# The last two pairs of heads of a stage share a matrix product, and the first pair of the next stage moves three products ahead

## The chip, the core and the metric

The kernel runs on one core of a Trainium2 chip. The metric is the device time of one execution in microseconds (us); lower is better. The core has a matrix engine (TensorE, PE in the profile; its weight loads are shown apart as PEld), a vector engine (VectorE, DVE), a scalar engine (ScalarE, ACT), GpSimd (POOL, idle here) and SyncE (SP), whose queue issues all DMA transfers. The engines run side by side and wait for each other through semaphores; within one engine the instructions run in the order in which the program lists them.

## What is computed

```python
# attention: q, k, v of shape (8, 12, 448, 64); sigmoid in place of softmax
scores = scale * q @ k.T - log(S)
attn_out = sigmoid(scores) @ v
x = attn_out, heads joined: (8 * 448, 768)
# feed-forward (FFN)
h = x @ w_in                     # 768 -> 2048
g = maximum(0.01 * h, h)
out = g @ w_out                  # 2048 -> 768
```

The weights arrive as 64-bit numbers and are turned to 32-bit ones on the chip.

## The kernel before

**Attention.** The 12 heads of 8 batches are handled as 48 pairs of heads, 12 pairs (two batches) to a stage; a pair's two heads sit on partitions 0 to 63 and 64 to 127. `Pair.scores(h)` (L336) makes two of four chunks of the transposed scores, in three matmuls for each head, since every operand of a product is split into a high and a low part; ScalarE applies the sigmoid to each chunk. `Pair.attn_v(h)` (L359) multiplies two chunks by v into one bank of the accumulator memory (PSUM), and `keep` (L379) copies the result into `xs`, where the 12 pairs of a stage fill four quarters `x(0)` to `x(3)` of three pairs each.

**Alone or joint.** `part(i)` (L40) says how the 448 keys of a pair are cut. Part 0, alone: four chunks of 112 rows, so v takes 8 matrix products. Parts 1 and 2 are two neighbouring pairs taken jointly: three chunks of 128 rows each, and the last 64 rows of both pairs sit in one tile, the first pair's on the lower and the second's on the upper partitions. The second pair's `attn_v(1)` (L369) makes the four small products of the shared tile for both pairs, and both pairs' `keep` come after it. In each of the stages 1 to 3 the pairs 0 to 9 of the stage are joint and the pairs 10 and 11 alone (`JOINT`, L36). In a trace each of these products stands as two matmuls.

**FFN, first half.** `First(p)` (L472) multiplies the result of attention stage p by `w_in`. Rows and columns are halved, and seven products (n = 0, 1, 4, 5, 3, 6, 2) of sums and differences of the halves take the place of eight; for eight column groups u that makes 56 products p0 to p55, of nine matmuls each. While stage q of the attention runs (q = 1 to 3), these are the products of stage q - 1; those of the last stage follow alone. Product n of group u accumulates in one of two PSUM banks, `px` and `pz`; `First.after` and `Quad.done` (L191) empty the bank by a copy on ScalarE (n = 0, 4, 5, 2) or an addition on VectorE (n = 1, 3, 6), and the product after next needs that bank. In the group u = 7 the sums of n = 3 and 2 are in `pz` and that of n = 6 is in `px`; n = 0 of the next group begins in `px`.

**Operands.** `Operands` (L385) makes the seven left operands from `x(0)` to `x(3)`: `s` entries are sums or differences on VectorE, `h` entries casts on ScalarE, `l` entries the differences that leave the low part, on VectorE. `PLAN` (L433) says ahead of which slot each comes: "h422" is the cast for product 4, pairs 2 to 2 of the quarter; "np2" is product 2 of the next stage. The weights of a product are cast by ScalarE three products ahead and get their low part from VectorE two products ahead (`advance`, L453).

**Slots.** `slot` (L112) first issues the chores that are due, those marked `first` ahead, and then the slot's matrix work; `later(n, ...)` puts a chore n slots on. `go` (L552) adds the entries of the plans, and, unless `busy` is set, `prepare` lets the conversion of the weights on VectorE (`prep`, L246) go one or two instructions on. With a pair come the casts of q and k of the pair after next, the load of v of the next pair, and a load of q and k for the pair four on (`next_parts`, L545).

**Order in a stage.** Ahead of each pair's slot run e{j}.0 (half its scores), e{j}.1 and e{j}.2 (v of the pair before it), e{j}.3 (the other half), and then 5, 5 or 4 products:

```python
            go(q, f"e{j}.0", (lambda: pairs[i].scores(0)) if q < NQ else None, busy)
            for h in range(2):
                go(q, f"e{j}.{1 + h}", lambda: pairs[i - 1].attn_v(h), busy)
            go(q, f"e{j}.3", (lambda: pairs[i].scores(1)) if q < NQ else None, busy)
```

So v of the last pair of a stage comes at e0 of the next one, after p55. After stage 3 the banks are dealt out anew (`ps_f`, three each for `px` and `pz`), and the remaining 56 products run without attention; then comes the second half of the FFN (`px_o`, `py_o`, `pz_o`).

Of the kernel before, what the change touches and what calls it, by code (L numbers as in the profile page):

```python
# [20 lines left out]
NOP = len(ORDER)  # L21
# [7 lines left out]

PACES = 1.5, 1.2, 0.9  # L30
WAIT = 5
PRODUCTS = 5, 5, 4


JOINT_ALONE = 1, 3, 5, 7
JOINT = 0, 2, 4, 6, 8  # L36
PER = 12


def part(i):  # L40

    q, j = divmod(i, PER)
    firsts = JOINT if q else JOINT_ALONE
    return 1 if j in firsts else 2 if j - 1 in firsts else 0
# [12 lines left out]
def attn_ffn_kernel(ctx: ExitStack, tc: tile.TileContext, qk, v, w_in, w_out, out):  # L57
# [19 lines left out]
    NU = w_in.shape[0]  # L77
    HW = NC // 2 * P
    NB = NC // 2
    NQ = B // 2  # L80
# [27 lines left out]
    def later(slots, *fns, first=False):  # L108

        chores.setdefault(now + slots, ([], []))[not first].extend(fns)  # L110

    def slot(work=None):  # L112
        nonlocal now
        for fns in chores.pop(now, ()):
            for fn in fns:
                fn()
        if work is not None:
            work()
        now += 1
# [93 lines left out]
    def banks(name, sizes):  # L213

        pool = ps.enter_context(tc.tile_pool(name=name, bufs=1, space=PSUM, reuse_waits="tile"))

        def psum(tag, name):
            bufs, n = sizes[tag]
            return pool.tile([P, n, 512] if n > 1 else [P, 512], F32, tag=tag, name=name, bufs=bufs)

        return psum
# [75 lines left out]
    def prepare():  # L297
        nonlocal credit
        credit += PACES[0] if (0, ALONE - 1) not in prepared else PACES[1] if (0, NU - 1) not in prepared else PACES[2]
        while credit >= 1:  # L300
            next(preps, None)
            credit -= 1
# [82 lines left out]
    class Operands:  # L385
# [45 lines left out]


    PLAN = {  # L433
# [4 lines left out]
    PLAN_ALONE = {  # L438
# [14 lines left out]
    def advance(t):  # L453

        nonlocal at_load, at_high, at_low
        while at_high < len(w1) and w1[at_high][0] <= t + 3:
            w1[at_high][1].high()
            at_high += 1
        while at_low < len(w1) and w1[at_low][0] <= t + 2:
            w1[at_low][1].low()  # L460
            at_low += 1
        while at_load < len(w1) and w1[at_load][0] <= t + 8 and at_load < at_low + len(w1_stage):
            x = w1[at_load][1]
            x.stage = w1_stage[-1]
            x.load()
            at_load += 1
# [61 lines left out]
    per = 2 * NP  # L528
    last = B * NP - 1
    pairs = [Pair(i) for i in range(B * NP)]  # L530
# [11 lines left out]
    first, ops = None, None  # L542
    psum = banks("ps_a", dict(s=(3, 2), pv=(2, 1)))

    def next_parts(i):  # L545
        if i + 2 <= last:
            later(1, pairs[i + 2].high)
            later(2, pairs[i + 2].low)
        if i + 4 <= last:
            later(4, pairs[i + 4].load_qk)  # L550

    def go(q, where, work, busy=False):  # L552


        for x, plan, key in ((ops, PLAN, where), (before, PLAN if q > 1 else PLAN_ALONE, "n" + where)):
            if x is not None:
                for what in (PLAN_ALONE if q == 0 and x is ops else plan).get(key, "").split():
                    later(0, lambda x=x, what=what: x.do(what))
        slot(work)
        if not busy:  # L560
            prepare()

    for q in range(NQ + 1):
        before, ops = ops, Operands(q) if q < NQ else None
        if q == 0:
            slot(lambda: pairs[0].scores(0))
        elif q == 1:
            ps.close()
            psum = banks("ps_b", dict(s=(2, 2), pv=(2, 1), px=(1, 1), pz=(1, 1)))
        k = 0  # L570
        for j in range(per if q < NQ else 1):
            i = q * per + j
            if q == 0 and 0 < j:
                later(0, pairs[i + 1].load_v)
            if q == 0:
                busy = j >= per - 2
                go(q, f"e{j}.0", lambda: pairs[i].scores(1), busy)
                next_parts(i)
                if j + 1 < per:
                    go(q, f"e{j}.1", lambda: pairs[i + 1].scores(0), busy)  # L580
                    for h in range(2):
                        go(q, f"e{j}.{2 + h}", lambda: pairs[i].attn_v(h), busy)
                if j >= per - 4:
                    for t in range(2):
                        advance(2 * (j - per) + t)
                continue
            if j == 0:
                first = First(q - 1, before)
            busy = j == 0 or j == per - 1 or q == NQ
            go(q, f"e{j}.0", (lambda: pairs[i].scores(0)) if q < NQ else None, busy)  # L590
            for h in range(2):
                go(q, f"e{j}.{1 + h}", lambda: pairs[i - 1].attn_v(h), busy)
            go(q, f"e{j}.3", (lambda: pairs[i].scores(1)) if q < NQ else None, busy)
            if q < NQ:
                next_parts(i)
                if i < last:
                    later(1, pairs[i + 1].load_v)
                for _ in range(PRODUCTS[j % len(PRODUCTS)]):
                    go(q, f"p{k}", first.step, busy or j == per - 2 and k >= 50 or k < 7)
                    k += 1  # L600
    ps.close()


# [150 lines left out]
```

## Time and profile before

| | us |
|---|---|
| median of three runs (lowest to highest) | 1109.43 (1107.17 to 1110.66) |
| the profiled execution | 1107.88 |
| its span, first to last instruction | 1106.1 |
| TensorE busy | 1094.2 |
| VectorE busy | 651.4 |
| ScalarE busy | 617.6 |

The stages in that execution: attention alone up to about 84 us; the stages 1 to 3 with 56 products each, from 84.06, 256.73 and 428.96 us, and v of the last pair up to 598.36 us; the products of the last stage up to 699 us; then the second half of the FFN. Between the execution's time and its span lie 1.8 us, ahead of the first and behind the last instruction. In a timeline a row begins with its start and its length in us. A matmul's length runs on into the next one's start, so the time that a block takes is read from start to start.

### The profile page before, as it was taken

The numbers are of one execution on the slowest core, as the hardware profiler recorded it, in microseconds if no ns is written. First come the engines' busy times: TensorE is split into PE (matmuls) and PEld (weight loads), VectorE is DVE, ScalarE is ACT, GpSimd is POOL, SyncE is SP. The second block draws the span as 40 slices with busy tenths as digits, with TensorE's granted clock in tenths as the row PEclk, the third lists the DMA queues.
The fourth block names the chain that finished last, engine by engine and source line by source line (L and its number), as shares of the span: only waits on it lengthen the run. The fifth ranks groups of instructions, "written<-read, shape, count | busy, mean of one in ns | idle before, by whom it ended". The sixth has DMA issues, their size and how long they took to land.

```text
span 1106.1 us, 15810 instructions
## 1 busy us (share of the span) xinstructions
PE 1094.2 (99%) x5952; PEld 895.1 (81%) x5952; DVE 651.4 (59%) x886; ACT 617.6 (56%) x883; POOL 0.3 (0%) x5
## 2 busy tenths in 40 slices
PE   8999999999999999999999999999999999999998
PEld 4547777777777777777777999999999999999998
DVE  5978777677666677666648666665433333343332
ACT  6897665677666668666667555554333233323331
POOL 0000000000000000000000000000000000000000
PEclk9999999999999999999999999999999999999999
DMA  8975888875878776788745889786655554454442
GB/s 289 326 249 189 311 284 284 310 254 185 264 273 289 275 234 211 242 274 292 242 151 177 264 270 297 268 280 214 206 147 150 158 175 150 133 177 150 156 149 93
DMA packets 101436, 250.08 MB, mean 226 GB/s; under 512 B 11280, under 2 KB 53904, under 8 KB 101360
## 3 DMA queue, kind: packets, MB, share of 16 engines
q1 hardware_dynamic: 101360, 249.08, 68.3%
q8 instruction: 46, 0.75, 0.3%
q14 instruction: 30, 0.25, 0.1%
HBM read 164.63 MB, written 84.41 MB: 225 GB/s over the span
## 4 chain that ended last, share of the span: by engine, by line
PE 95%; ACT 2%; DMA 1%; DVE 1%; issue 0%; SPq 0%; ACTq 0%
PE px_o L90 21%; PE px_h L90 21%; PE pv L90 11%; PE pz_h L90 11%; PE sc L90 11%; PE pz_o L90 10%; PE py_o L90 5%; PE py_h L90 5%; ACT s L90 1%; ACT so L90 1%; DMA v<-in_v 1%; DMA qk<-in_qk 0%; ACT qks L90 0%; DVE wd L90 0%; DVE so L90 0%
## 5 line engine op out<-in xcount | busy, mean ns | idle before, releaser
L90 DVE TENSOR_TENSOR gs<-gg,gs 128x896 fp32r<-128x896 f32 x112 | 122.4, 1092 | 226.8 <-ACT gs L90 226.7
L90 PE MATMUL px_h<-so,w 128*128 128x448 f32 x1152 | 249.7, 363 | 0.2 <-ACT c_h L90 0.2
L90 PE MATMUL px_o<-gs,w 128*128 128x448 f32 x1152 | 232.5, 362 | 0.0
L90 PEld LDWEIGHTS px_h<-so,w 128*128 128x128 f32 x1152 | 214.8, 187 | 19.7 <-issue 3.0
L90 ACT CAST gs<-gg 128x896 fp32r<-128x896 f32 x112 | 105.6, 943 | 221.7 <-PE px_o L90 116.1
L90 PEld LDWEIGHTS px_o<-gs,w 128*128 128x128 f32 x1152 | 216.0, 187 | 14.4
L90 ACT ACTIVATE s<-sc 128x896 f32<-128x896 f32 (+1 forms) x192 | 171.5, 917 | 59.4 <-PE sc L90 35.0
L90 PE MATMUL sc<-qks 64*128 64x448 f32 (+2 forms) x1152 | 144.7, 386 | 8.0 <-ACT qks L90 4.6
L90 DVE TENSOR_TENSOR w<-wx,w 128x768 fp32r<-128x768 f32 (+1 forms) x160 | 136.1, 853 | 26.8 <-ACT w L90 26.3
L90 PEld LDWEIGHTS sc<-qks 64*128 64x128 f32 (+2 forms) x1152 | 98.3, 180 | 65.5 <-issue 28.2
L90 PE MATMUL pv<-s,v 128*64 128x448 f32 (+2 forms) x768 | 144.1, 551 | 0.2 <-DMA v<-in_v 0.2
L90 PE MATMUL pz_h<-so,w 128*128 128x448 f32 x576 | 128.3, 367 | 0.0
L90 ACT CAST w<-wx 128x768 fp32r<-128x768 f32 (+1 forms) x160 | 119.9, 753 | 6.2 <-DMA wx<-t 6.1
L90 PEld LDWEIGHTS pz_h<-so,w 128*128 128x128 f32 x576 | 106.2, 188 | 14.8 <-issue 7.0
L90 PE MATMUL pz_o<-gs,w 128*128 128x448 f32 x576 | 116.5, 362 | 0.0
L90 PEld LDWEIGHTS pz_o<-gs,w 128*128 128x128 f32 x576 | 108.0, 187 | 7.2
L90 PEld LDWEIGHTS pv<-s,v 128*64 128x64 f32 (+2 forms) x768 | 44.0, 136 | 78.3 <-issue 77.4
L90 ACT COPY c_h<-px_h 128x448 f32<-128x448 f32 x64 | 34.1, 533 | 68.6 <-PE px_h L90 68.5
L90 PE MATMUL py_h<-so,w 128*128 128x448 f32 x288 | 62.8, 362 | 0.0
L90 DVE TENSOR_TENSOR qks<-qk,qks 128x896 fp32r<-128x896 f32 (+1 forms) x49 | 52.3, 1068 | 17.1 <-ACT qks L90 16.9
L90 DVE SCALAR_TENSOR_TENSOR wd<-wr,wd 128x768 int32<-128x768 int32 x64 | 61.2, 956 | 1.1
L90 ACT ACTIVATE c_h<-c_h 128x448 f32<-128x448 f32 x96 | 55.4, 577 | 10.1 <-DVE c_h L90 9.8
(37 smaller groups left out, 660.8 us busy)
## 6 DMA issues: line engine op xcount, KB each, us to landing
gg<-g SPq DMA_DIRECT2D x112, 448.0 KB, 3.5
wx<-t SPq DMA_DIRECT2D x120, 384.0 KB, 3.9
g<-c_h SPq DMA_DIRECT2D x128, 224.0 KB, 4.4
g<-s SPq DMA_DIRECT2D x96, 224.0 KB, 4.4
qk<-in_qk SPq DMA_DIRECT2D x47, 448.0 KB, 4.9
wr<-in_w_in SPq DMA_DIRECT2D x16, 768.0 KB, 7.1
t<-ws SPq DMA_DIRECT2D x16, 768.0 KB, 7.1
wr<-in_w_out SPq DMA_DIRECT2D x16, 768.0 KB, 5.9
```

Of the source, the lines that this page charges most:

```text
L90: return lambda *args, **kw: tc.keep_in_program_order(issue(*args, **kw))
```

## The change

The list of joint pairs gains pair 10, so that pairs 10 and 11 of the stages 1 to 3 are taken jointly. The pairs are placed among the 56 products by one formula in place of 5, 5 and 4: in stage 1 thirteen pairs go ahead of the products 0, 4, 9, 13, 18, 22, 26, 31, 35, 40, 44, 49 and 53, the thirteenth (e12) being the first pair of stage 2 with v of the last of stage 1. The stages 2 and 3 begin at e1, ahead of the products 2, 6, 11, 16, 20, 25, 30, 34, 39, 44, 48 and 53. At e12 of stage 3 there are no further scores, and only v of the last pair is left. The plan of the operands follows: entries for the pairs 1 to 2 of a quarter are joined ("h412", "s212"), and they run from p50 to np3, where they ran from p50 to np5. The slots e11 no longer count as busy; e12 does.

```diff
-PRODUCTS = 5, 5, 4
-JOINT = 0, 2, 4, 6, 8
+JOINT = 0, 2, 4, 6, 8, 10
+AHEAD_OF = 3
     PLAN = {
-        "p21": "h002", "p22": "l002", "p48": "s302", "p50": "h102", "p51": "l102 h502", "e11.0": "l502",
-        "e11.1": "s200", "e11.2": "h400", "e11.3": "l400", "p52": "s211 h411", "p53": "l411 s101",
-        "p54": "h301 l301", "p55": "h601 s401", "ne0.0": "l601 h201", "ne0.1": "l201", "ne0.3": "s222",
-        "np0": "h422 l422", "np1": "s122 h322", "np2": "l322 h622", "np3": "l622 s422", "np4": "h222", "np5": "l222"}
+        "p21": "h002", "p22": "l002", "p48": "s302", "p50": "h102", "p51": "l102 h502", "p52": "l502 s200",
+        "e12.0": "h400", "e12.1": "l400", "e12.3": "s212", "p53": "h412 s102", "p54": "l412 h302", "p55": "l302 s402",
+        "np0": "h602", "np1": "l602", "np2": "h202", "np3": "l202"}
@@ the loop over the stages, for q above 0 @@
-            busy = j == 0 or j == per - 1 or q == NQ
-                for _ in range(PRODUCTS[j % len(PRODUCTS)]):
-                    go(q, f"p{k}", first.step, busy or j == per - 2 and k >= 50 or k < 7)
-                    k += 1
+        first = First(q - 1, before)
+        if q == NQ:
+            break
+
+        size = NU * NOP
+        spread = (size - AHEAD_OF, 0) if q == 1 else (size, AHEAD_OF)
+        places = {round(j * spread[0] / per) - spread[1]: j for j in range(q > 1, per + 1)}
+        for k in range(size):
+            j = places.get(k)
+            if j is not None:
+                i, busy = q * per + j, j in (0, per)
+                go(q, f"e{j}.0", (lambda: pairs[i].scores(0)) if i <= last else None, busy)
+                for h in range(2):
+                    go(q, f"e{j}.{1 + h}", lambda: pairs[i - 1].attn_v(h), busy)
+                go(q, f"e{j}.3", (lambda: pairs[i].scores(1)) if i <= last else None, busy)
+                if i <= last:
+                    next_parts(i)
                 if i < last:
                     later(1, pairs[i + 1].load_v)
+            go(q, f"p{k}", first.step, k >= 50 or k < 7)
```

## Rows read from the trace of the kernel before

**Rows 1.** The page, parts 1 and 2: busy time by engine; the granted clock.
```profile
PE 1094.2 (99%) x5952; PEld 895.1 (81%) x5952; DVE 651.4 (59%) x886; ACT 617.6 (56%) x883; POOL 0.3 (0%) x5
...
PEclk9999999999999999999999999999999999999999
```

**Rows 2.** Windows, stage 1: length; busy PE, PEld, DVE, ACT, POOL; clock, DMA share, GB/s.
```profile
84.06:256.73 172.67, 172.49 (x986) 128.39 (x984) 131.45 (x193) 117.90 (x174) 0.00 (x0) 1.00 0.81 272
```

**Rows 3.** Timeline of PE, 252 to 286 us: start, length, work, tile, matmuls.
```profile
252.16 3.23 PE L90 MATMUL pv<-s,v 112*64 112x448 f32 x16
255.32 1.48 PE L90 MATMUL sc<-qks 64*128 64x448 f32 x12
256.73 2.08 PE L90 MATMUL px_h<-so,w 128*128 128x448 f32 x9
258.65 1.96 PE L90 MATMUL py_h<-so,w 128*128 128x448 f32 x9
260.45 1.96 PE L90 MATMUL px_h<-so,w 128*128 128x448 f32 x9
...
267.37 2.48 PE L90 MATMUL pv<-s,v 128*64 128x448 f32 x12
269.77 1.50 PE L90 MATMUL sc<-qks 64*128 64x448 f32 x12
...
281.84 3.39 PE L90 MATMUL pv<-s,v 128*64 128x448 f32 x20
285.15 1.48 PE L90 MATMUL sc<-qks 64*128 64x448 f32 x12
```

**Rows 4.** Timeline of PE and ACT, 87 to 92 us: products p2 to p4 of stage 1.
```profile
89.57 1.96 PE L90 MATMUL pz_h<-so,w 128*128 128x448 f32 x9
...
91.15 0.52 ACT L90 COPY c_h<-px_h 128x448 f32<-128x448 f32 x1
...
91.72 2.08 PE L90 MATMUL px_h<-so,w 128*128 128x448 f32 x9 [0.18 <-ACT c_h L90]
```

**Rows 5.** Groups of instructions by form: count, busy us, mean ns, idle before.
```profile
L90 ACT ACTIVATE s<-sc 128x896 f32<-128x896 f32 x114 | 104.2, 919 | 49.9 <-PE sc L90 30.8 <-PE pv L90 18.9
L90 DVE TENSOR_TENSOR w<-wx,w 128x768 fp32r<-128x768 f32 x120 | 113.9, 952 | 2.2 <-ACT w L90 2.1
L90 DVE TENSOR_TENSOR so<-x,so 128x896 fp32r<-128x896 f32 x12 | 13.0, 1085 | 0.0
L90 ACT CAST so<-x 128x896 fp32r<-128x896 f32 x12 | 11.2, 945 | 1.3 <-DVE x L90 1.2
L90 DVE TENSOR_TENSOR x<-x,x 128x1344 f32<-128x1344 f32 x4 | 6.2, 1551 | 0.0
```

**Rows 6.** Timeline, 590 to 599 us: DVE behind p52 to p54, keep after v.
```profile
590.45 1.08 DVE L90 TENSOR_TENSOR x<-x,x 128x896 f32<-128x896 f32 x1
...
591.46 0.55 DVE L90 TENSOR_TENSOR w<-wx,w 128x384 fp32r<-128x384 f32 x1
...
591.92 0.61 DVE L90 TENSOR_TENSOR c_h<-c_h,px_h 128x448 f32<-128x448 f32 x1
...
598.36 2.07 PE L90 MATMUL px_h<-so,w 128*128 128x448 f32 x9
598.47 0.54 ACT L90 COPY x<-pv 128x448 f32<-128x448 f32 x1 [1.33 <-PE pv L90]
```

**Rows 7.** Timeline, 601 to 604 us: a weight's low part beside its product.
```profile
601.37 0.95 DVE L90 TENSOR_TENSOR w<-wx,w 128x768 fp32r<-128x768 f32 x1
...
602.07 1.99 PE L90 MATMUL px_h<-so,w 128*128 128x448 f32 x9
```

**Rows 8.** Timeline of DVE and PE, 185 to 191 us: conversion waits for a transfer.
```profile
185.88 0.56 DVE L90 TENSOR_SCALAR wd<-wr 128x768 int32<-128x768 int32 x1 [2.48 <-DMA wr<-in_w_in]
...
186.71 3.78 PE L90 MATMUL px_h<-so,w 128*128 128x448 f32 x18
...
187.70 0.62 DVE L90 TENSOR_TENSOR c_h<-c_h,pz_h 128x448 f32<-128x448 f32 x1
```

More of the change, by code (lines that the diff above doesn't have):

```diff
@@ L569, in attn_ffn_kernel @@
             psum = banks("ps_b", dict(s=(2, 2), pv=(2, 1), px=(1, 1), pz=(1, 1)))
[L570 to L576, printed above, removed]
+        if q == 0:
+            for j in range(per):
+                i, busy = j, j >= per - 2
+                if 0 < j:
+                    later(0, pairs[i + 1].load_v)
                 go(q, f"e{j}.0", lambda: pairs[i].scores(1), busy)
@@ L585, in attn_ffn_kernel @@
                         advance(2 * (j - per) + t)
-                continue
-            if j == 0:
-                first = First(q - 1, before)
-            busy = j == 0 or j == per - 1 or q == NQ
[L590 to L595, printed above, removed]
+            continue
+        first = First(q - 1, before)
[14 more added lines that the diff above has]
+                    next_parts(i)
                 if i < last:
                     later(1, pairs[i + 1].load_v)
-                for _ in range(PRODUCTS[j % len(PRODUCTS)]):
-                    go(q, f"p{k}", first.step, busy or j == per - 2 and k >= 50 or k < 7)
-                    k += 1
+            go(q, f"p{k}", first.step, k >= 50 or k < 7)
     ps.close()
```

## The prediction

> **What bounds the kernel now.** I read the page's engine shares first: TensorE is busy 99% of the span, at full granted clock in all 40 slices (2.4 GHz), while VectorE and ScalarE are busy little over half of it [rows 1]. So the end moves with TensorE's own work and with waits put into its queue. The windows by stage come next: stage 1 lasts 172.67 us, and TensorE is busy for 172.49 of them, VectorE for 131.45 and ScalarE for 117.90 [rows 2]. Idle time there is next to nothing, so I went on to the timeline of TensorE, from start to start: half a pair's scores take 256.73 - 255.32 = 1.41 us, the first product behind them 258.65 - 256.73 = 1.92, a product that follows another 260.45 - 258.65 = 1.80 [rows 3]. The only held product that I found in the stages 1 to 3 is p4 of stage 1: due at 89.57 + 1.80 = 91.37, it starts at 91.72, right behind a copy of ScalarE that ends at 91.15 + 0.52 = 91.67 and frees its bank [rows 4]. There is thus about 0.4 us of waiting to win back, and the rest must come from less work on TensorE.
>
> **What the joint pairs take away.** v of an alone pair takes 255.32 - 252.16 = 3.16 us. Of a joint two, the first takes 269.77 - 267.37 = 2.40 and the second 285.15 - 281.84 = 3.31 [rows 3]. Two pairs alone are 6.32, two joint 5.71: 0.61 less, in three stages 1.83 us, all of it on the path. The scores cost the same 24 matmuls either way, and the number of changes between pairs and products stays (37 insertions in both orders), so neither has a term.
>
> The first of a joint two makes three column pairs in 2.40, or 0.80 each; the eight half-height matmuls of the second add 3.31 - 2.40 = 0.91, so the shared chunk costs 0.11 more than a column pair [rows 3]. The Trainium skill, "TensorEngine Tiling (Array Packing)", section "Key Properties", says that a change of tiling mode drains the array, which speaks against a fourth chunk of another shape in two more pairs of each stage. By its section "Theoretical Speedup" alone, without that drain, seven units of 3.16 / 4 = 0.79 would take the place of eight, and three stages would gain 2.4.
>
> **What the earlier pair moves.** Placed by the formula, e1 of stage 1 comes behind four products, not five, so that it lies between p3 and p4: 2 x 1.41 + 2.40 us of other matrix work cover the copy that p4 waited for, and the 0.35 us go [rows 3, 4]. The moved pair (e12) issues its own chores three products earlier: casts of q and k of the pair after next (a cast of ScalarE and a subtraction of VectorE over 896 columns, 0.95 and 1.09), one load of v and one of q and k on SP's queue. Nobody waits for these for at least one whole insertion (5 us and more), so I cost them at nothing but their place in VectorE's queue, below. The four slots of e11 now let the weight conversion go on: the same instructions, some earlier.
>
> **The new waits.** What remains is the operand work at the end of a stage. In the kernel before, v of the last pair came with e0, between p55 and np0, and its pieces were spread over six products. Now it stands between p52 and p53, and quarter 3 is finished as one piece of two pairs: "s212", then "s102", "l412", "l302", "s402", and in between them the additions that free banks. VectorE takes these in order. The rows behind p52 show the pattern: a sum over 896 columns, a weight's low part, then the addition that frees the bank of n = 3 [rows 6]. An instruction there holds the engine 0.07 to 0.09 less than its length (the next starts at 591.46 and 591.92) [rows 6]; so I count 1.47 for 1344 columns (1.55 long), 1.01 for 896, 0.87 for 768, 0.46 for 384 and 0.53 for an addition of 448 [rows 5, 6].
>
> End of stage 3, where e12 has no scores; time 0 is the end of v, when p53 starts. The first keep starts 0.11 later (598.47 against 598.36) and takes 0.54 [rows 6]; there are two now, to 1.19. VectorE: s212 to 2.20, s102 to 3.67, the low part of a weight (384) to 4.13, and only then the addition for p53, which ends at 4.13 + 0.61 = 4.74. It frees the bank that p55 adds to; p55 is due at 1.92 + 1.80 = 3.72. **Wait 1.0 us.** Then l412 to 5.67, a weight to 6.54, an addition to 7.07, l302 to 8.54, s402 to 10.01, and the low part of the weight of np2 ends at 10.96. np2 is due at 4.74 + 3 x 1.80 = 10.14, but the low part is read by the third of its nine matmuls: in the kernel before it ended at 601.37 + 0.95 = 602.32, after that product's start at 602.07, and the product was 1.99 long against 1.96 elsewhere [rows 3, 7]. So it is due at 10.54. **Wait 0.4 us.** A sum, l602, an addition and a sum follow, then the low part for np4, which ends at 14.9 and is due at 14.56. **Wait 0.3 us.** Together 1.75.
>
> End of the stages 1 and 2, where e12 has scores behind v: they push p53 back by 1.41, so p55 is safe (addition at 4.74, due at 5.13). But np0 follows p55 at once and needs the bank that the addition for p54 frees: l412 to 5.67, a weight to 6.54, the addition ends at 7.15, due at 1.41 + 1.92 + 2 x 1.80 = 6.93. **Wait 0.2 us, twice.** ScalarE is not the late one: two keeps, two sigmoids (0.92 each) and the cast "h412" (0.95) end near 4.0, ahead of l412's turn at 4.66 [rows 5]. Behind np0 comes np1 and then e1, 5 us of attention in which both queues catch up.
>
> The trace of before has no such joined piece, so these waits are bounded: 0 if VectorE or the bank is quicker by the sum of its terms, and about twice as long if every piece is also held up once by a late cast; I take the sum, as all its terms are rows. Before, the same stretch showed no wait, since e0 lay between p55 and np0.
>
> **The sum.** -1.83 - 0.35 + 0.44 + 1.75 = 0.0 us. The profiled execution took 1107.88, 1.55 under the median of 1109.43, and lies inside the runs' 1107.17 to 1110.66. I forecast no change: about 1107.9 for an execution like the profiled one, 1109.4 for a median.
>
> **Rivals.**
> *The waits don't come*: nothing at the ends of stages is late, and the gain stays: -1.83 - 0.35 = -2.2, a median of 1107.2. For it: no row of before shows a product held there. Against it: four terms of VectorE's queue are rows, and they end behind the time that is due.
> *VectorE is held by transfers (slower)*: in stage 1 twelve pairs now share 53 products, not 56, and the conversion of weights runs in the same queue. It waited 2.48 us for a transfer at 185.88, and the addition behind it ended at 187.70 + 0.62 = 188.32, while the product that needs the bank started at 186.71 + 1.80 = 188.51 [rows 8]. Only 0.19 us were left. From a queue longer by 0.2 on, all of such a wait falls on TensorE: 2.3 us for one, and with as much at two places and the sum above, +4.6, a median of 1114.0. For it: VectorE is at 76% in stage 1, the most of any stage. Against it: the wait moves with the slots, and most places have more room.
> *The joint form gains nothing here*, as the pairs 10 and 11 are followed by a joint pair at once and ScalarE's tiles run out: the 1.83 is lost, a median of 1111.2. Against it: joint pairs follow each other at pairs 0 to 9 already, with no wait.
>
> **How the numbers follow.** No change as summed, within 1 us: 0.62. The gain without the waits: 0.20. The slower rival: 0.11. The joint form without gain: 0.07. A measurement of this kernel tells about 0.3% (3.3 us) from no change. All cases but the slower rival at its full size lie within that, and the scatter of medians adds a little at either side: faster 0.04, same 0.88, slower 0.08. The range reaches from the second case, less half of what the runs scatter, 1106.3, to the fourth with the same on top, 1112.6; beyond it are the slower rival and a few odd medians, under 2 in 10.
>
> **What the profile of the changed kernel would show.** v of the pairs 10 and 11 at 2.40 and 3.31; p4 of stage 1 no longer behind a copy; p55 of stage 3 about 1 us late behind an addition of VectorE, np2 and np4 of the last stage a little late behind a weight's low part, np0 of the stages 2 and 3 by 0.2. The stages 1 to 3 together some 1.8 us shorter in matrix work, and that much idle in TensorE's row near 595 us. The forecast is wrong if the addition for p53 comes ahead of "s102", if a product inside a stage waits behind a conversion of weights, or if TensorE waits for a load.

## The result, and the profile after

| | before | after |
|---|---|---|
| median of 22 runs each, same chip, us | 1109.51 | 1111.22 |
| lowest to highest | 1107.17 to 1111.56 | 1109.94 to 1112.84 |
| the profiled execution; its span | 1107.88; 1106.1 | 1110.19; 1108.1 |

The ratio is 1.0017 (1.0012 to 1.0023): the changed kernel is 1.7 us slower. That is less than 0.3%, but the interval leaves 1 out, so the forecast of no change did not hold. One run of those in the next section, of the kernel with the last quarter in two pieces, took 1860.79 us at a granted clock of 0.62 and is left out of its median.

Part 1 of the page of after answers to [rows 1]:

```profile
PE 1093.6 (99%) x5952; PEld 892.6 (81%) x5952; DVE 648.6 (59%) x865; ACT 618.4 (56%) x871; POOL 0.3 (0%) x5
```

TensorE is busy for 0.6 us less, and the span is 2.0 us longer: less matrix work, more waiting. To set kernels side by side I take the stretch from p0 of stage 1 to the second half of the FFN, in which every kernel here does the same products. The windows of before, then of after (columns as in [rows 2]):

```profile
84.06:699.30 615.24, 615.06 (x3435) 478.04 (x3434) 427.61 (x627) 403.16 (x610) 0.00 (x0) 1.00 0.76 253
```

```profile
83.72:701.25 617.53, 615.60 (x3435) 476.89 (x3434) 425.13 (x606) 404.34 (x598) 0.00 (x0) 1.00 0.76 252
```

The stretch is 617.53 - 615.24 = 2.29 us longer. To find where, I went through TensorE's timeline from start to start and noted each block that takes longer than the usual steps of [rows 3] (1.80 between products, 1.92 behind attention, 1.41 for scores, 2.40, 3.31 or 3.16 for v). What is over is called held below. Before has 0.46 us of it, all at p4 of stage 1; after has 4.41. Against that stands the matrix work saved, which can be seen at the end of stage 3, where pair 10 takes 578.74 - 576.34 = 2.40 and pair 11 takes 592.69 - 589.38 = 3.31. The timeline of PE of after, first p3 to p4 of stage 1, then the end of stage 3:

```profile
89.23 1.96 PE L90 MATMUL pz_h<-so,w 128*128 128x448 f32 x9
91.12 1.49 PE L90 MATMUL sc<-qks 64*128 64x448 f32 x12
...
96.36 2.07 PE L90 MATMUL px_h<-so,w 128*128 128x448 f32 x9
...
576.34 2.48 PE L90 MATMUL pv<-s,v 128*64 128x448 f32 x12
578.74 1.50 PE L90 MATMUL sc<-qks 64*128 64x448 f32 x12
...
589.38 3.39 PE L90 MATMUL pv<-s,v 128*64 128x448 f32 x20
592.69 2.08 PE L90 MATMUL px_h<-so,w 128*128 128x448 f32 x9
```

p4 of stage 1 (96.36) now follows a pair and is not held, where it waited behind a copy before [rows 4]. Summed over the stretch, v takes 103.03 us in after and 104.81 in before, and the halves of the scores ahead of it 49.57 against 49.46: 1.67 us less matrix work. The balance is -1.67 - 0.46 + 4.41 = +2.28, against 2.29 measured. The 4.41 us lie at these places (a held product makes the one behind it some 0.1 us late too; that is added in):

| place in after | held, us | what the product waits for |
|---|---|---|
| p55 of stage 3 | 1.02 + 0.11 | addition for p53, behind the sums of quarter 3 |
| np0 of the stages 2 and 3 | 2 x (0.30 + 0.09) | addition for p54, same queue |
| np2 and np4 behind stage 3 | 0.41, 0.34 | low part of a weight, same queue |
| np6 behind stage 3 | 0.23 + 0.11 | addition for np4, behind the low part l202 |
| p17 and p24 of stage 1 | 0.65, 0.42 | an addition in VectorE's queue, behind a conversion that waited |
| p24 of stage 2 | 0.34 | an addition behind the low part l002 |

The first four lines are the ends of stages, 3.00 us; the last two lie inside the stages, 1.41 us.

The end of stage 3 in the timeline of after (PE, ACT and DVE), answering to [rows 6]:

```profile
592.81 0.97 ACT L90 COPY x<-pv 128x448 f32<-128x448 f32 x2 [1.31 <-PE pv L90]
593.82 1.09 DVE L90 TENSOR_TENSOR s<-x,x 128x896 f32<-128x896 f32 x1 [1.66 <-ACT x L90]
594.83 1.55 DVE L90 TENSOR_TENSOR x<-x,x 128x1344 f32<-128x1344 f32 x1
596.29 0.55 DVE L90 TENSOR_TENSOR w<-wx,w 128x384 fp32r<-128x384 f32 x1
596.76 0.61 DVE L90 TENSOR_TENSOR c_h<-c_h,px_h 128x448 f32<-128x448 f32 x1
597.43 3.88 PE L90 MATMUL px_h<-so,w 128*128 128x448 f32 x18 [0.85 <-DVE c_h L90]
```

The chain is the one that was foretold: two keeps, a sum over 896 columns, one over 1344, a weight, and only then the addition, which ends at 597.37. That is 4.68 behind the end of v at 592.69; 4.74 was worked out.

The end of stage 1 in the same timeline (PE, DVE, and PEld for the weights of np0):

```profile
254.76 4.15 PE L90 MATMUL px_h<-so,w 128*128 128x448 f32 x18
...
256.10 0.61 DVE L90 TENSOR_TENSOR c_h<-c_h,pz_h 128x448 f32<-128x448 f32 x1
...
256.83 0.71 PEld L90 LDWEIGHTS px_h<-so,w 128*128 128x128 f32 x4 [0.48 <-ACT c_h L90]
```

The first row is p55 and np0 in one. np0 was due at 254.76 + 1.80 = 256.56; the addition for p54 ends at 256.71, and the first weights of np0 are loaded at 256.83. (The work that the row names as releaser had ended before, and the addition is the nearest event.)

Inside stage 1, the timeline of SP, DVE and PE of after:

```profile
119.49 0.33 SPq L90 DMA_DIRECT2D t<-ws  x1
...
127.28 0.56 DVE L90 TENSOR_SCALAR wd<-wr 128x768 int32<-128x768 int32 x1 [2.42 <-DMA t<-ws]
...
129.69 1.08 DVE L90 TENSOR_TENSOR qks<-qk,qks 128x896 fp32r<-128x896 f32 x1
129.89 1.96 PE L90 MATMUL px_h<-so,w 128*128 128x448 f32 x9
...
131.56 0.61 DVE L90 TENSOR_TENSOR c_h<-c_h,py_h 128x448 f32<-128x448 f32 x1
...
132.22 2.08 PE L90 MATMUL pz_h<-so,w 128*128 128x448 f32 x9 [0.37 <-DVE c_h L90]
```

The conversion of a weight block waits until the store of the block before it has landed (t<-ws, 119.49 to 127.28), with everything behind it in VectorE's queue. The addition that frees the bank ends at 132.17; p17 was due at 129.89 + 1.80 = 131.69. In the kernel before, VectorE waits equally long at this point, and nobody is held (timeline of SP, DVE and PE of before):

```profile
121.30 1.91 SPq L90 DMA_DIRECT2D t<-ws  x1
...
127.11 0.56 DVE L90 TENSOR_SCALAR wd<-wr 128x768 int32<-128x768 int32 x1 [2.40 <-DMA t<-ws]
...
131.05 0.61 DVE L90 TENSOR_TENSOR c_h<-c_h,py_h 128x448 f32<-128x448 f32 x1
131.58 1.08 DVE L90 TENSOR_TENSOR qks<-qk,qks 128x896 fp32r<-128x896 f32 x1
...
132.49 1.96 PE L90 MATMUL pz_h<-so,w 128*128 128x448 f32 x9
```

The wait is the same, 2.40 against 2.42, but two other things differ. One is the order behind it: there the subtraction for q and k (1.08) comes behind the addition, and with the pairs at their new places it comes ahead of it. The addition ends 131.66 - 127.11 = 4.55 behind the conversion's start there and 132.17 - 127.28 = 4.89 here, as a sum over 448 columns that stands in between there (0.62) stands elsewhere here; the order thus accounts for 0.34. The other is the store: from its issue to the conversion it took 127.11 - 121.30 = 5.81 there and 127.28 - 119.49 = 7.79 here, 1.98 more. In the kernel before the addition ended only 132.49 - 131.66 = 0.83 ahead of p17, so by these rows a store as long as here would have held p17 there too (an estimate; no run has it). It is the longer store that makes p17 late; the new order adds 0.34 to it.

### The profile page after: what moved, and what is told of

It is laid out like the page before. It is cut to its first block, busy times and chain, and to the rows that moved or that the text cites. A ratio compares the mean times of both kernels' runs of the same rounds, so it can differ in the third digit from the quotient of the medians.

```text
span 1108.1 us, 15826 instructions
## 1 busy us (share of the span) xinstructions
PE 1093.6 (99%) x5952; PEld 892.6 (81%) x5952; DVE 648.6 (59%) x865; ACT 618.4 (56%) x871; POOL 0.3 (0%) x5
## 4 chain that ended last, share of the span: by engine, by line
PE 90%; DVE 4%; DMA 2%; ACT 2%; issue 1%; SPq 0%; DVEq 0%; ACTq 0%
PE px_o L90 21%; PE px_h L90 19%; PE pv L90 11%; PE pz_o L90 10%; PE sc L90 10%; PE pz_h L90 10%; PE py_o L90 5%; PE py_h L90 5%; DMA qk<-in_qk 2%; DVE wd L90 1%; DVE qks L90 1%; DVE c_h L90 1%; ACT s L90 1%; DVE w L90 1%; DMA g<-s 1%
```

## The experiments

The theory: the time went to two things, VectorE's joined pieces at the ends of stages, and additions pushed behind conversions and low parts inside them. The rivals: that the joint pairs gain nothing, and that the move of e12 by itself costs the time. Medians stand beside runs of the kernel before on the same chip, and the stretch is the one above. Held time comes from the same count as the 4.41. Of the lines of `PLAN` the diffs show only entries near a change.

**The last quarter in two pieces.** Sums and casts of the first two pairs' part ahead of v, so that only the rest is behind it:

```diff
-"p52": "l502 s200", "e12.0": "h400", "e12.1": "l400", "e12.3": "s212", "p53": "h412 s102",
-"p54": "l412 h302", "p55": "l302 s402", "np0": "h602", "np1": "l602", "np2": "h202", "np3": "l202"
+"p52": "l502 s200", "e12.0": "h400 s100", "e12.1": "l400 h300", "e12.2": "l300 s400", "e12.3": "s212",
+"p53": "h412", "p54": "s112 h312", "p55": "l412", "np0": "l312 h602", "np1": "l602 s412",
+"np2": "h202", "np3": "l202"
```

> The changed kernel with the operand work at the end of a stage cut in pieces: column 0 of quarter 3 is handled while v of the last pair still runs, and the sum over the other two columns comes behind the addition that frees the bank of p53. Theory A (the waits at the ends of stages are VectorE's queue ahead of bank-freeing additions): p55 of stage 3 is no longer held (1.0 us in the changed kernel), nor np0 of the stages 2 and 3 (0.3 each with its tail) nor np2 of the last stage (0.4); about 0.4 us at np4 stay; 2.0 us less than the changed kernel, near 1109.2, level with the kernel before or 0.3 under it. Rival B (those products are held by something else that the move brings, a transfer or a cast): the waits stay and the time is that of the changed kernel, 1111.2.

Measured: 1109.29 us against 1109.30, ratio 0.9999 (0.9990 to 1.0008); stretch 615.43, 2.10 less than after. The waits at the ends of the stages are gone, and one came up new: 0.71 at np4 of the last stage, where the copy that frees the bank stands on ScalarE behind the cast h202, which waits for s412. At p24 of stage 1 the hold grew from 0.42 to 1.17, and p17 is free (its store took 7.22, see the table below). So the ends were worth what they showed, and the time inside stages is another matter.

**The conversions two slots later**, for two of the weight blocks:

```diff
-                yield from (None for _ in range(WAIT))
+                yield from (None for _ in range(WAIT + 2 * (m in (5, 6))))
```

> The changed kernel, but the conversions of the sixth and seventh block of weights begin two calls later, so that the store of the block before has more time to land. Theory A (inside stage 1 VectorE sits in front of a conversion until that store has landed, 2.4 us at 127 us and 3.9 at 153, and the bank-freeing additions wait behind): both idle times shrink to under 1 us, p17 and p24 of stage 1 are held no longer, 1.0 us less than the changed kernel. Rival B (the products there are held because the pairs stand denser, whatever the transfers do): VectorE's idle time goes, but p17 and p24 stay late, and the time is that of the changed kernel.

Measured: 1112.32 us, ratio 1.0031 (1.0020 to 1.0043); stretch 619.94, 2.41 more than after. A miss: p17 and p24 of stage 1 are free as expected, but the wait came back at p34 of stage 1, as 2.52 + 0.12, and p24 of the stages 2 and 3 is held for 0.86 and 0.33. The timeline of PE and DVE of this kernel:

```profile
184.04 1.96 PE L90 MATMUL pz_h<-so,w 128*128 128x448 f32 x9
186.62 0.56 DVE L90 TENSOR_SCALAR wd<-wr 128x768 int32<-128x768 int32 x1 [3.76 <-DMA t<-ws]
187.69 0.61 DVE L90 TENSOR_TENSOR c_h<-c_h,px_h 128x448 f32<-128x448 f32 x1
188.36 1.88 PE L90 MATMUL px_h<-so,w 128*128 128x448 f32 x8 [2.36 <-DVE c_h L90]
```

VectorE stands idle for 3.76 us ahead of a conversion, with the addition queued behind it. Of this wait 2.52 us fall on TensorE. Putting these conversions off moved the wait and did not remove it.

**A cast and its low part two products later**, so that the low part (1344 columns) comes behind the addition at p24:

```diff
-"p21": "h002", "p22": "l002"
+"p23": "h002", "p24": "l002"
```

> The changed kernel, but the cast and the low part of the first operand of the next stage (1344 columns each) come at p23 and p24, not at p21 and p22. Theory A (in stage 2, p24 is held 0.3 us because this low part stands in VectorE's queue together with the conversions, two products after a pair): that wait goes, 0.3 us less; in stage 1, where a transfer is the cause, p24 stays late or the wait moves. Rival B: p24 of stage 2 stays 0.3 us late.

Measured: 1110.92 us in one run; stretch 616.62, 0.91 less than after. p24 is held in neither stage, though VectorE idles for 3.96 us ahead of 154.65. The 0.42 + 0.34 are gone, in stage 1 too, where the expectation had left it open, and p17 and the ends stand as in after. DVE and PE in the timeline, at p24 of stage 2 in after and then at p24 of stage 1 here:

```profile
326.85 1.56 DVE L90 TENSOR_TENSOR so<-x,so 128x1344 fp32r<-128x1344 f32 x1
327.44 1.98 PE L90 MATMUL px_h<-so,w 128*128 128x448 f32 x9
...
328.80 0.61 DVE L90 TENSOR_TENSOR c_h<-c_h,py_h 128x448 f32<-128x448 f32 x1
329.46 2.08 PE L90 MATMUL pz_h<-so,w 128*128 128x448 f32 x9
```

```profile
154.65 0.56 DVE L90 TENSOR_SCALAR wd<-wr 128x768 int32<-128x768 int32 x1 [3.96 <-DMA t<-ws]
156.52 1.96 PE L90 MATMUL px_h<-so,w 128*128 128x448 f32 x9
156.79 0.62 DVE L90 TENSOR_TENSOR c_h<-c_h,py_h 128x448 f32<-128x448 f32 x1
158.32 1.96 PE L90 MATMUL pz_h<-so,w 128*128 128x448 f32 x9
```

With the low part ahead, the addition ends at 329.41 and the product starts at 329.46, due at 329.24. With the low part behind, it ends at 157.41, 0.9 us early, despite the idle time.

**All three edits together** (the diffs above).

> The three edits together: the operand work in pieces, the two conversions later, the first operand at p23 and p24. If the waits that were found (4.4 us in the changed kernel) are all that the change costs, 3.5 to 4.0 us go: 1107.2 to 1107.7, about 2 us under the kernel before, which is what the shared product saves by the matmuls (1.8) with the wait at p4 of stage 1 gone. If the shared product saves nothing on the path, it ends near 1109.5, level with the kernel before.

Measured: 1110.29 us, ratio 1.0007 (0.9999 to 1.0015); stretch 615.88. A miss: p34 of stage 1 is held for 2.00, from the later conversions, and np4 of the last stage for 0.72, from the two pieces. Two of the edits brought waits of their own.

**The two that help, with h202 later**: the two pieces with "h202" and "l202" at np3 and np4, h002 and l002 at p23 and p24, and the conversions as in after.

> The changed kernel with the operand work in pieces (as in the run with pieces, and the cast of the last operand two products later, since it held the copy for p3 of the last stage there) and the first operand at p23 and p24; the conversions as in the changed kernel. Theory A (the change costs only the products held behind VectorE, 4.4 us): all but the wait of 0.6 at p16 of stage 1 and some 0.4 at p4 of the last stage go, 3.4 us less than the changed kernel: 1107.8, some 1.6 under the kernel before. Rival B (the shared product gains nothing on the path): level with the kernel before, 1109.4.

Measured: 1107.45 us against 1108.68, ratio 0.9988 (0.9980 to 0.9997): faster than before, by little. Its windows and, below, the end of stage 3 in DVE's and PE's timeline:

```profile
83.68:697.92 614.24, 613.99 (x3434) 477.16 (x3433) 426.11 (x615) 404.49 (x601) 0.00 (x0) 1.00 0.76 253
```

```profile
590.78 2.08 PE L90 MATMUL px_h<-so,w 128*128 128x448 f32 x9
592.92 0.55 DVE L90 TENSOR_TENSOR w<-wx,w 128x384 fp32r<-128x384 f32 x1
593.39 0.61 DVE L90 TENSOR_TENSOR c_h<-c_h,px_h 128x448 f32<-128x448 f32 x1
593.92 1.08 DVE L90 TENSOR_TENSOR x<-x,x 128x896 f32<-128x896 f32 x1
594.50 3.76 PE L90 MATMUL px_h<-so,w 128*128 128x448 f32 x18
```

The addition for p53 now comes ahead of the second sum, ends 3.22 behind the end of v (594.00 against 590.78) and holds nobody. What is held in the stretch falls from 4.41 to 1.22, or 3.19 less, and the stretch is 617.53 - 614.24 = 3.29 shorter. Of this 0.65 is p17, which this execution does not hold at all: its store took 6.42 (see the table below), and no edit did that. At p24 of stage 1 nobody is held behind a wait of 4.68 us, where after waits 3.85 us ahead of its conversion at 152.98 and holds p24 for 0.42:

```profile
153.11 0.56 DVE L90 TENSOR_SCALAR wd<-wr 128x768 int32<-128x768 int32 x1 [4.68 <-DMA t<-ws]
```

The Trainium skill, "Perfetto Trace Analysis", section "Optimizing Scalar/DVE Operations", says that an engine which isn't saturated but leaves others idle may be helped by breaking its instructions up. Here the shorter pieces do that: what is left behind v is 896 columns in place of 1344.

**The same with one conversion one slot later** (`WAIT + (m == 5)`).

> The kernel of the run best, but the conversions of the sixth block of weights begin one call later. Theory A (p16 of stage 1 is held because VectorE sits in front of a conversion for a store that has not landed): its idle time at 128 us shrinks from 2 us to 1 or less and p16 is held no longer, 0.5 us less; the blocks after it move on by a call, so a wait of up to 2 us may come up at another product. Rival B (density of the pairs): p16 stays late.

Measured: 1107.94 us, ratio 0.9990 (0.9981 to 0.9999); stretch 614.24, held 1.23, as without it. VectorE's idle time ahead of p17 was 1.92 us against 1.06. The expectation (its p16 is p17 in the count used here) took over the hold seen in after; in best p17 was not held, so that there was nothing to win and the run does not test the theory.

**The move without the joint pairs:**

```diff
-JOINT = 0, 2, 4, 6, 8, 10
+JOINT = 0, 2, 4, 6, 8
```

> The changed kernel with pairs 10 and 11 alone again; order and plan as changed. Theory A (the shared product saves 0.61 us a stage on the path, and the operand work behind it costs more because two results come at once): 1.8 us more of matrix work, while p55 of stage 3 is held 0.6 in place of 1.0 us and np0 of the stages 2 and 3 hardly at all; 0.7 us more than the changed kernel, 1111.9. Rival B (joint pairs gain nothing on the path): 1.2 us less than the changed kernel, 1110.0.

Measured: 1111.41 us against 1108.68, ratio 1.0023 (1.0014 to 1.0032); stretch 617.73. p55 of stage 3 is held for 0.58 + 0.11, np0 not at all, p24 of stage 1 for 0.87. Held in all: 3.00, or 1.41 less than after, and still the stretch is 0.20 longer. So the loss comes with the new places and the plan that goes with them, which this run does not tell apart, and the joint pairs win back 1.61 of it.

**The best kernel without the joint pairs** (the same line taken back).

> The kernel of the run best, but pairs 10 and 11 alone again, so that the shared product is priced where next to nothing waits at the end of a stage. Theory A (0.61 us a stage, all on the path): 1.8 us more than the run best. Rival B (the shared product gains nothing on the path, since the drain at its change of shape or its late result takes it back): the time of the run best, within 0.5 us.

Measured: 1110.09 us against 1108.81, ratio 1.0008 (0.9999 to 1.0017). Its windows:

```profile
85.89:702.32 616.43, 616.01 (x3435) 477.86 (x3433) 425.62 (x614) 404.75 (x601) 0.00 (x0) 1.00 0.76 252
```

The stretch is 616.43 - 614.24 = 2.19 longer, of which 0.44 is held time (0.41 at p17 of stage 1). The remaining 1.75 is the matrix work. The rival that the joint pairs gain nothing falls. Against the kernel before, the stretch is 616.43 - 615.24 = 1.19 longer, and held time, 1.66 against 0.46, accounts for it: with the better plan, too, the move loses time without the joint pairs. The Trainium skill, "TensorEngine Tiling (Array Packing)", section "Key Properties", has the drain at a change of tiling mode; 2.4 was the sum without a drain, and the runs lie below it. That the drain is the difference, no run here shows.

**The joint pairs without the move**: the order of before, `JOINT` with 10, and the last two pairs of a quarter as one piece, spread over six products:

```diff
-JOINT = 0, 2, 4, 6, 8
+JOINT = 0, 2, 4, 6, 8, 10
-"p52": "s211 h411", "p53": "l411 s101", "p54": "h301 l301", "p55": "h601 s401", "ne0.0": "l601 h201",
-"ne0.1": "l201", "ne0.3": "s222", "np0": "h422 l422", "np1": "s122 h322", "np2": "l322 h622",
-"np3": "l622 s422", "np4": "h222", "np5": "l222"
+"p52": "s100", "p53": "h300", "p54": "l300 h600", "p55": "l600 s400", "ne0.0": "h200",
+"ne0.1": "l200", "ne0.3": "s212", "np0": "h412 l412", "np1": "s112 h312", "np2": "l312 h612",
+"np3": "l612 s412", "np4": "h212", "np5": "l212"
```

> The kernel before with pairs 10 and 11 joint in the stages 1 to 3 and its plan of operands fitted to it (both results come after p55, so s212 follows e0, then the operands of pairs 1 and 2 of the quarter; column 0 ahead of that), without moving a pair. Theory A (the waits come from how late the operands of the last two pairs stand in VectorE's queue): 1.8 us less matrix work, but np2 to np4 of the next stage are held about 1 us in the stages 2 and 3 and np2 to np6 2 us in the last one; about 2 us more than the kernel before, 1111. Rival B (the new order of the pairs is what costs, and the shared product is free): 1.8 us less than the kernel before, 1107.4.

Measured: 1111.57 us, ratio 1.0022 (1.0013 to 1.0031); stretch 618.29, 3.05 more than before. Held: 5.30, with some 0.97 at np2 to np4 of each of the stages 2 and 3, 2.02 behind stage 3, 0.89 at p35 and 0.47 at p4 of stage 1. 5.30 - 0.46, less the 1.67 to 1.83 of the matrix work, is 3.0 to 3.2. With this plan and without the earlier pair the joint pairs finish the quarter too late, so the move does buy something: the room in which best can finish the quarter.

**One more operation on VectorE** ahead of s102, in the stages 1 to 3 (a maximum of a tile with itself, 1344 columns, which leaves the values as they are):

```diff
+            if self.p:
+                vec(out=self.x(2)[:, a:b], in0=self.x(2)[:, a:b], in1=self.x(2)[:, a:b], op=ALU.max)
             add(self.x(2)[:, a:b], self.x(2)[:, a:b], self.x(3)[:, a:b])
```

> The changed kernel with one more VectorE instruction over 1344 columns ahead of s102 (the larger of a value and itself, so nothing is changed by it) in the stages 1 to 3. Theory A (at p53 to p55 VectorE's queue is the path): 1.47 us in each of three places come out in full at p55 and np0, less the slack of p55 in the stages 1 and 2 in part: p55 of stage 3 held 2.5 us, p55 of the stages 1 and 2 held 1.0 and np0 behind it 0.6 in place of 0.3; 4 us more, near 1115.4. Rival B (the end of the stages is held by ScalarE or by transfers): 1111.2 as in the changed kernel.

Measured: 1116.80 us, ratio 1.0073 (1.0057 to 1.0088); stretch 622.62, 5.09 more than after, where some 4 us were expected. DVE and PE at the end of stage 3:

```profile
599.16 1.97 PE L90 MATMUL pz_h<-so,w 128*128 128x448 f32 x9
599.38 1.55 DVE L90 TENSOR_TENSOR x<-x 128x1344 f32<-128x1344 f32 x1
600.97 1.56 DVE L90 TENSOR_TENSOR x<-x,x 128x1344 f32<-128x1344 f32 x1
602.91 0.61 DVE L90 TENSOR_TENSOR c_h<-c_h,px_h 128x448 f32<-128x448 f32 x1
603.58 4.69 PE L90 MATMUL px_h<-so,w 128*128 128x448 f32 x15 [2.45 <-DVE c_h L90]
```

p55 of stage 3 is held for 2.61, or 1.59 more: the 600.97 - 599.38 = 1.59 us of the operation, start to start, in full. In the stages 1 and 2, p55 is held for 1.20 and np0 for 0.69 + 0.09, also 1.59 more for each stage; there p55 had slack and np0 stood behind it, and together they still take the whole operation. So what p55 and np0 wait for is VectorE's queue, one for one.

That makes 3 x 1.59 = 4.77. The rest is of another kind. Behind the idle time of 2.45 us ahead of p55 of stage 3 the granted clock fell to 0.50, the lower of its two levels (1.2 GHz), and the matmuls came 0.37 us apart in place of 0.20 (windows of this kernel, columns as in [rows 2]):

```profile
605.10:608.40 3.30, 3.30 (x10) 2.94 (x9) 3.30 (x4) 2.21 (x3) 0.00 (x0) 0.50 0.31 99
```

Up to np1 this costs 1.70 us, where after has 0.11; np2, np4 and np6 are then no longer held (1.09 less), and inside the stages 0.15 less is held: 4.77 + 1.59 - 1.09 - 0.15 = 5.1.

## Why the prediction was wrong, point by point

*Matrix work of the joint pairs, -1.83.* Right in kind, 0.16 too large: the blocks are 2.40 and 3.31, and three comparisons give 1.61 (after and the move alone), 1.75 (best with and without) and 1.79 (the joint pairs alone: 5.30 - 0.46 - 3.05). Summed over the blocks of the stretch it is 1.67: v gains 1.78, since the 0.61 a stage came from lengths rounded to 0.01, and half the scores of a pair take 1.39 us ahead of an alone v but 1.41 or 1.42 ahead of a joint one, 0.11 in all, which had no term.

*p4 of stage 1, -0.35.* Right, and 0.11 more, since the product behind the held one was late as well.

*The ends of stages.* The mechanism was right at each place named, and the largest term to the hundredth: 1.0, 0.4 and 0.3 came as 1.02, 0.41 and 0.34. Mis-sized: np0 of the stages 2 and 3 at 0.30, not 0.2, since it starts 0.15 behind the addition and not at once, and the tail of 0.1 behind a held product, which I had not counted (0.11 and 2 x 0.09). Missed: np6 behind stage 3, 0.34, held by an addition behind the low part that I had counted up to np4 only. Together 3.00 where 2.19 was summed.

*The step that failed* is "What the earlier pair moves". It says "Nobody waits for these for at least one whole insertion ..., so I cost them at nothing but their place in VectorE's queue" and looks at the chores of the moved pair alone; the new places of all other pairs inside the stages have no term beyond p4. The work itself did cost nothing. But with the pairs at other products, additions that free banks came behind work that was not due yet, and products inside the stages were held for 1.41 us. Of these 0.76, at p24 of the stages 1 and 2, are the order in VectorE's queue: the low part l002 over 1344 columns stood ahead of the addition, and with l002 two products later both holds are gone. The other 0.65, at p17, are a conversion that waits for a store, with the addition behind it. The sum had 0.0 in place of the 1.41 and so came out at 0.0 in all: -1.83 - 0.35 + 2.19. With what was measured it is -1.67 - 0.46 + 3.00 + 1.41 = +2.28: besides the 1.41 that had no term, the ends were 0.81 too small. The rows to see the 1.41 were there: I looked at one place where a conversion holds the queue [rows 8] and took the other places to have more room.

Of the 1.41, the 0.65 at p17 of stage 1 are a matter of one execution in good part: seven of the kernels have the same program up to p17, and its wait differs between them.

| kernel | store's issue to conversion, us | p17 held for, without its tail |
|---|---|---|
| after | 127.28 - 119.49 = 7.79 | 0.53 |
| low part later | 128.84 - 121.14 = 7.70 | 0.45 |
| one more operation | 128.73 - 121.04 = 7.69 | 0.44 |
| best, pair 10 alone | 129.24 - 121.69 = 7.55 | 0.30 |
| two pieces | 128.04 - 120.82 = 7.22 | 0 |
| move alone | 126.64 - 119.69 = 6.95 | 0 |
| best | 125.88 - 119.46 = 6.42 | 0 |

Up to 7.25 us the store costs nothing; beyond that every tenth falls on TensorE (7.79 - 0.53, 7.70 - 0.45, 7.69 - 0.44 and 7.55 - 0.30 are all 7.25 or 7.26). Part of what best shows against after in one profile is thus the store, not the edit. In the two kernels with the old places the same store took less: 5.81 in before, and 125.92 - 121.17 = 4.75 with the joint pairs without the move. Why it takes longer with the new places, no run shows. The hold at p24 of stage 2 is not of this kind: with l002 at p22 it stood in all five kernels, and with l002 at p24 in none of five.

*The rivals.* "The waits don't come" fell. "VectorE is held by transfers" was the right mechanism in the right stage, at a lower price than its 2.3 us for a wait, as the additions had some room left; a little above that price (2.52) and about its named place (186.6 us) it appeared when the conversions were put off. What VectorE waits for at these places is the store of a block, where [rows 8] had a load. "The joint form gains nothing" fell with best and its version without pair 10.

*The bound of a measurement.* I counted 0.3% as what a measurement can tell. With 22 runs on either side the interval is 0.0011 wide, and 1.7 us are told from nothing. The ends of the range do not follow from the words beside them either: half of what the runs scatter is (1110.66 - 1107.17) / 2 = 1.7, which gives 1105.5 and 1112.9, not 1106.3 and 1112.6.

## What to carry to other kernels

When instructions are put at other places of an in-order queue, go through every point where that queue waits for a transfer, and compare the order behind it with the old order: what frees a buffer of the bounding engine should stand ahead of what is not due yet. Here a wait of 4.68 us on an engine at 59% load cost nothing with the low part behind the addition, and one of 3.85 us cost 0.42 with the low part ahead of it. Beyond the room that is left, such a wait cost its length (the 7.25 of the table). One profile does not tell how long a transfer takes the next time: ask how much longer it may take before somebody is held. Moving work earlier paid here only when what became ready was taken in pieces short enough for the additions between them.

## What the runs showed of the hardware

A store of 768 KB, issued at a busy DMA (share 0.76 over the stretch), took between 6.42 and 7.79 us until VectorE went on, in the same program at the same place (the table above). The Trainium skill, "Perfetto Trace Analysis", section "DMA Instruction — HWDGE (DVE, Sync)", says that a transfer's semaphore is updated only once the write is confirmed, with a delay that can surprise when the target is HBM; the rows show the whole from issue to use, and not what share of it is that confirmation.

TensorE's granted clock fell in the attention stage ahead of p0 in some executions and not in others. TensorE had idled for 1.8 us behind a sigmoid at about 78 us in both kernels below; then, from 80 to 84 us, the granted clock was a mean 0.66 in the one, which is made of both its levels (1.2 GHz is 0.5, 2.4 GHz is 1.0; from 79.30 to 82.71 us it was 0.50), and 1.00 in the other. Windows of best without pair 10, then of best (columns as in [rows 2]):

```profile
76.00:80.00 4.00, 2.19 (x20) 1.18 (x16) 2.78 (x5) 4.00 (x8) 0.00 (x0) 0.91 0.69 216
80.00:84.00 4.00, 4.00 (x16) 1.40 (x16) 1.52 (x3) 2.59 (x4) 0.00 (x0) 0.66 0.22 87
```

```profile
76.00:80.00 4.00, 2.20 (x18) 1.04 (x16) 2.73 (x5) 4.00 (x7) 0.00 (x0) 1.00 0.60 167
80.00:84.00 4.00, 4.00 (x28) 1.81 (x25) 2.67 (x5) 3.22 (x5) 0.00 (x0) 1.00 0.21 79
```

In the first, 16 matmuls were done in 80 to 84 us, in the second 28, and p0 of stage 1 starts at 85.89 against 83.68. Of the twelve profiled executions five have the lower clock there, and their p0 starts at 85.04 to 85.89; in the other seven it starts at 83.61 to 84.21. This is a scatter of some 1.5 us that no edit here touched, and the reason why the stretch from p0 on compares kernels more sharply than single times do. The times agree: of the kernel before, 16 runs beside best have a mean granted clock of 0.999 or 1.00 and a median of 1108.24 us, and 11 have 0.998 and 1110.05; best has 1106.90 (7 runs) and 1108.60 (4), so it is the faster one at either clock.

Inside the stretch the clock fell in one of the twelve profiled executions, the kernel with one more operation, behind 2.45 us of idle time (0.50 from 605.10 to 608.40 us). Behind the 2.36 us of idle time at p34 where the conversions were put off, it stayed at 1.00.
